# First batch of a threshold attention with a two-layer MLP: the softmax divisors reach x^T through DRAM instead of through TensorE

## The chip, the cores and the metric

The kernel runs on one core of a Trainium2 chip. The metric is the device time of one execution in microseconds (us), as the median of several runs. The core's engines are TensorE (PE; its weight loads are shown apart as PEld), VectorE (DVE), ScalarE (ACT), GpSimd (POOL) and SyncE (SP), which only issues DMA transfers here. ACT and POOL can issue transfers too. Each engine works through its own instructions in order.

## The reference

Attention with 8 batches, 8 heads, 576 positions and 64 channels a head. In each row of scores only those within `tau` of the row's maximum count; the softmax's divisor is the sum over these. The result, with the heads side by side, is the input x (4608 tokens, 512 channels) of an MLP with 2048 hidden channels and an exact GELU.

```python
scores = scale * np.matmul(q, k.transpose(0, 1, 3, 2))
thresh = np.max(scores, axis=-1, keepdims=True) - tau
scores = np.where(scores >= thresh, scores, -1000000000.0)
scores = scores - np.max(scores, axis=-1, keepdims=True)
attn = np.exp(scores)
attn = attn / (np.sum(attn, axis=-1, keepdims=True) + 1e-09)
attn_out = np.matmul(attn, v)
x = attn_out.transpose(0, 2, 1, 3).reshape(B * S, H * D)
h = x @ w_in
out = (0.5 * h * (1.0 + erf(h / sqrt(2)))) @ w_out
```

## The kernel before, in words

Everything is float32. The two heads of a pair stand side by side, so a batch has four pairs and the kernel 32. The 576 query positions of a pair are cut into four chunks of 128 and a tail of 64; the tails of both heads share one chunk, chunk 4.

For each chunk, `scores` (L410) has PE compute scores into PSUM. `softmax_head` takes the negated maximum of each row on DVE (`nmx`, L422), lets POOL work out the threshold (`thr`, L423), and ACT the exponential (`p`, L425). `softmax_tail` has DVE zero what lies below the threshold and sum the rest in the same instruction (L442); the sum goes to `den` in the first batch, and to a column of `sums` later. The exponentials are turned (in the first batch on PE, L356, and copied by ACT, L363; later by DVE and by regrouping transfers on SP, L528 and L524), and `weigh_v` or `weigh_half` multiplies them by v on PE (L545, L569). Its result is x^T: channels on the partitions, tokens along the row. ACT copies it into a block of 256 tokens (`xall`, L555, L571).

So the product with v is taken before the division. The divisors are one per row and lie on the partitions, while x^T has its tokens along the row: they have to be turned, and spread over the 64 channels of a head. The kernel has two ways for that.

In the first batch (`p < EARLY`, pairs 0 to 3) POOL adds 1e-9 to the sums of a chunk (L445), DVE inverts them in the next step (`invert`, L451), and `divide_early` has PE multiply the column, repeated 64 times as the stationary operand, by the identity (L464). ACT copies the outcome from PSUM to `inv` (L466), and POOL multiplies the x^T block by it (L472). `divide_early` runs twice for a pair: for the first 256 tokens (chunks 0 and 1) and for the other 320.

In later batches `divisors` runs once for a pair: DVE adds 1e-9, inverts and turns `sums` (L480, L481, L483), and SP writes the outcome to DRAM (L486) and reads it back, each row repeated on 64 partitions, into `inv` (L492, L494). `divide` multiplies on POOL (L585).

The order of the work is written out by hand in one loop over (pair, chunk) steps. The first batch has 20 steps: first chunks 0 and 1 of pairs 0 to 3, then chunks 2, 3 and 4 of pairs 0 to 3. In each step the scores and the maxima come first, then what is due from earlier steps (weighing and dividing, two steps after the chunk's scores), then matmuls of the MLP as far as `fill` is told to go, then the turns and `softmax_tail`. A division of the first batch therefore stands two steps after the masking that gives its divisors.

Beside this the first batch converts the MLP's weights, which arrive as float64: POOL issues loads of 512 KB pieces (L183), ACT and DVE take the pieces apart (L202, L203, L210, L212), and POOL adds the halves (L226). POOL's queue so holds thresholds, these additions, weight loads and the multiplications by `inv`, in one order. SP's queue holds the loads of q, k and v for the first pairs (L288 to L299), then those of pairs 4 and 5 (`load(HP)` in the last step of pair 1, `load(HP + 1)` three steps ahead of the second batch; L260, L269), and later the regrouping. `load_v_early(p + 2)` stands in the step of chunk 0 of pairs 0 and 1.

`inv` is one buffer (`dg` has one), and so each filling waits until POOL has used the one before.

From about 140 us on there is always an MLP block for PE to fill its gaps with; the last ten blocks are left to the end (L825, `last_blocks`).

Of the kernel before, what the change touches and what calls it, by code (L numbers as in the profile page):

```python
# [8 lines left out]
FP32 = mybir.dt.float32  # L9
# [3 lines left out]
ALU = mybir.AluOpType  # L13
# [5 lines left out]
def kernel(  # L19
# [28 lines left out]
    nc = tc.nc  # L48
    ctx.enter_context(tc.manual_schedule())

    B, H, S, D = q.shape
    d_model, d_ff = moe_w_in.shape
    P = 128
    Q = 32
    HP = H // 2
    NP = B * HP
    EARLY = HP
    NC = S // P
    MAIN = NC * P
    TAIL = S - MAIN  # L60
# [5 lines left out]
    TOK = 256  # L66
# [6 lines left out]
    SLOTS = NC + 1  # L73
# [4 lines left out]
    small = ctx.enter_context(tc.tile_pool(name="small", bufs=4))  # L78
    dram = ctx.enter_context(tc.tile_pool(name="dram", bufs=1, space=bass.MemoryType.DRAM))
    ps = ctx.enter_context(tc.tile_pool(name="ps", bufs=4, space=PSUM))  # L80
# [12 lines left out]
    dg = late_end.enter_context(tc.tile_pool(name="dg", bufs=1))  # L93
# [27 lines left out]
    ident = const.tile([P, P], FP32, name="ident")  # L121
# [122 lines left out]
    st = {}  # L244
# [184 lines left out]
    def softmax_tail(p, i):  # L429

        s = st[p]
        sc, thr, w = s.pop(("sc", i)), s.pop(("thr", i)), s["p", i]
        n = len(sc)
        if p < EARLY:
            pair = small.tile([P, 2], FP32, tag="den", name="den", bufs=2 * SLOTS)
            den = [pair[:, e:e + 1] for e in range(n)]
        else:
            at = [e * NC + i if i < NC else 2 * NC for e in range(n)]
            den = [sums[p % 2][:, x:x + 1] for x in at]
        for e in range(n):  # L440
            row = w[:, e * S:(e + 1) * S].rearrange("p (h s) -> p h s", h=2)
            nc.vector.scalar_tensor_tensor(  # L442
                row, sc[e][:, :, 0:HALF], thr[:, e:e + 1], row, op0=ALU.is_ge, op1=ALU.mult, accum_out=den[e])
        if p < EARLY:
            nc.gpsimd.tensor_scalar(pair[:, 0:n], pair[:, 0:n], 1e-9, None, op0=ALU.add)  # L445
            s["sum", i] = pair[:, 0:n]

    def invert(p, i):

        den = st[p]["sum", i]  # L450
        nc.vector.reciprocal(den, den)  # L451

    def divide_early(p, lo, hi):


        s = st[p]
        b, hp = divmod(p, HP)
        tr = ps.tile([P, 512], FP32, tag="mm", name="tr")
        for i in range(lo // P, -(-hi // P)):
            den = s.pop(("sum", i))  # L460
            to = tr[:, i * P - lo:min((i + 1) * P, hi) - lo]
            for e in range(2):
                one_of, cols = (den[:, e:e + 1], ident) if i < NC else (den, ident[:, e * TAIL:(e + 1) * TAIL])
                nc.tensor.matmul(to[e * D:(e + 1) * D, :], lhsT=one_of.to_broadcast([P, D]), rhs=cols, start=True, stop=True)  # L464
        by = dg.tile([P, S], FP32, tag="inv", name="inv")
        nc.scalar.copy(by[:, 0:hi - lo], tr[:, 0:hi - lo])  # L466
        for n, o, at, size in in_blocks(b, lo, hi):
            x, y = x_blk[n][:, hp, o:o + size], by[:, at - lo:at - lo + size]
            if size == TOK:
                x = x.rearrange("q (p c) -> q c p", c=2)  # L470
                y = y.rearrange("q (c p) -> q c p", c=2)
            nc.gpsimd.tensor_tensor(x, x, y, op=ALU.mult)  # L472

    def divisors(p):

        den = sums[p % 2]
        n = 2 * NC + 1
        nc.vector.tensor_scalar(den[:, 0:n], den[:, 0:n], 1e-9, None, op0=ALU.add)  # L480
        nc.vector.reciprocal(den[:, 0:n], den[:, 0:n])  # L481
        turned = small.tile([P, Q], FP32, tag="turned", name="turned", bufs=2)
        nc.vector.transpose(turned, den)  # L483
        eng = nc.gpsimd if p == NP - 1 else nc.sync
        rows = dram.tile([4, Q, Q], FP32, tag="turned", name="turned", bufs=4)
        eng.dma_start(rows.rearrange("a k i -> (a k) i"), turned)  # L486
        t = st[p]["inv"] = dg.tile([P, S], FP32, tag="inv", name="inv")
        flat = rows.rearrange("a k i -> a (k i)")
        for e in range(2):
            to = t[e * D:(e + 1) * D]  # L490
            src = flat[:, e * P:(e + 1) * P].unsqueeze(0).to_broadcast([D, 4, P])
            eng.dma_start(to[:, 0:MAIN].rearrange("p (a x) -> p a x", x=P), src)  # L492
            src = rows[2 * e:2 * e + 2, 2 * NC, :].unsqueeze(0).to_broadcast([D, 2, Q])
            eng.dma_start(to[:, MAIN:S].rearrange("p (a x) -> p a x", x=Q), src)  # L494
# [596 lines left out]
    for n in range(len(slots) + WEIGH + 1):  # L1091
        p, i = slots[n] if n < len(slots) else divmod(n, SLOTS)
        early = p < EARLY
        last = slots[n - 1] if 0 < n <= len(slots) else None
        if p < NP:
            scores(p, i)
            softmax_head(p, i)
            add_low_bits()
            if last and last[0] < EARLY:
                invert(*last)  # L1100
            if p < HP - 1 and i == 0:
                turn_qk_early(p + 1)
        elif n == len(slots):
            early_end.close()
            weights_first()
        gelus(0)
        if n == BATCH:
            gelus_held()
        table()
        for args in due:  # L1110
            if len(args) == 2:
                weigh_half(*args)
                if args[1]:
                    divide_early(args[0], 0, TOK)
                continue
            weigh_v(*args)
            divide_early(*args)
        due = []
        if p > EARLY and i == WEIGH:
            for lo, hi in (0, WIDE), (WIDE, S):  # L1120
                weigh_v(p - 1, lo, hi)
            if p == NP:
                divide(p - 1)
        owed += (goal(n) - goal(n - 1)) * BLK_NS * (PARTS[i] if not early and p < NP else 1.0)
        if early:
            fill(owed, tokens)
            owed = 0.0
            table()
        if last and last[0] < EARLY and last[1] < NC:
            turn_p_early(*last)  # L1130
        if p < NP:
            softmax_tail(p, i)
        if p < NP and not early:
            turn_p(p, i)
        if p < NP and not early:
            if i == 2:
                regroup(p, 1)
            if i > 2:
                regroup(p, i)
            if i == NC:  # L1140
                divisors(p)
        if last and last[0] < EARLY and last[1] == NC:
            turn_p_early(*last)
        if p < 2 and i == 0:
            for _ in range(2):
                load_piece()
            load_v_early(p + 2)
        if p == 1 and i == NC:
            load(HP)
        if n == BATCH - 3:  # L1150
            load(HP + 1)
        if n == BATCH:
            for t in pd_tail + [turned_p[:, e, h, :, :] for e in range(2) for h in range(2)]:
                nc.gpsimd.memset(t[:, NB:4 * KR, :], 0.0)
        if EARLY < p < NP and i == DIVIDE:
            divide(p - 1)
        if p >= HP and i == 1 and p + 2 < NP:
            loads = load_steps(p + 2)
        if p >= HP:
            next(loads, None)  # L1160
        if p >= HP and i == 1 and p + 1 < NP or p == HP - 1 and i == 2:
            scale_q(p + 1)
        if p >= HP - 1 and i == 2 and p + 1 < NP:
            turn_qk(p + 1)
        convert(0 if n == 0 else 1200 if n < 3 else 1900 if n < BATCH - 1 else 1e9)
        if not early:
            lag[0] = 2 if p < NP else 0
            if n != BATCH:
                share = 0.4 if n == BATCH + 1 else 1.0
                fill(owed * share, tokens)  # L1170
                owed *= 1.0 - share
        if n in BUSY:
            keep_busy(BUSY[n])
        if last and last[0] < EARLY:
            if last[1] < 2 and last[0] in HALVED:
                due.append((last[0], last[1]))
            elif last[1] == 1:
                due.append((last[0], 0, TOK))
            if last[1] == NC:
                due.append((last[0], TOK, S))  # L1180
        if n == START - 1:
            tokens = TOK
        elif n == BATCH + 1:
            tokens = S
        elif p > EARLY and i == DIVIDE and p % HP == 0 or p == NP and i == WEIGH:
            tokens = p // HP * S
            leaving += [n for n in AWAY if n in x_blk and (n + 1) * TOK <= tokens]
        elif leaving and i < 2:
            put_away(leaving.pop(0))
# [35 lines left out]
```

## Time and profile before

| | |
|---|---|
| Time, median of 3 runs | 1340.18 us (1338.49 to 1342.54) |
| The profiled execution | 1340.39 us, span 1338.6 us |
| Busy, share of the span | PE 99%, PEld 67%, DVE 78%, ACT 45%, POOL 49% |
| Chain that ended last | PE 93%, DVE 2%, the rest 1% or less each |
| L464, PE | 80 matmul records of 0.22 to 0.27 us, from 27.0 to 139.0 us |
| L466, ACT | 8 copies, 0.37 to 0.46 us |
| L445, POOL | 20 additions, median 0.30 us |
| L451, DVE | 20 reciprocals, 0.15 us |
| L472, POOL | 12 multiplications, median 0.76 us, from 28.5 to 142.6 us |
| `turned` to DRAM, SP (later batches) | 27 writes, median 1.9 us from issue to landing |
| `inv` from DRAM, SP (later batches) | 108 reads, median 4.0 us from issue to landing |

The span is the profiled execution from its first to its last instruction. A group of the profile names the line, the engine, the operation and the tiles; the chain that ended last follows the work back from the end, at each step to what released it. Times in the trace count from the start of the span.

### The profile page before, as it was taken

The numbers are of one execution on the slowest core, as the hardware profiler recorded it, in microseconds if no ns is written. First come the engines' busy times: TensorE is split into PE (matmuls) and PEld (weight loads), VectorE is DVE, ScalarE is ACT, GpSimd is POOL, SyncE is SP. The second block draws the span as 40 slices with busy tenths as digits, with TensorE's granted clock in tenths as the row PEclk, the third lists the DMA queues.
The fourth block names the chain that finished last, engine by engine and source line by source line (L and its number), as shares of the span: only waits on it lengthen the run. The fifth ranks groups of instructions, "written<-read, shape, count | busy, mean of one in ns | idle before, by whom it ended". The sixth has DMA issues, their size and how long they took to land.

```text
span 1338.6 us, 19954 instructions
## 1 busy us (share of the span) xinstructions
PE 1320.5 (99%) x6354; PEld 893.9 (67%) x6354; DVE 1043.3 (78%) x2005; ACT 604.9 (45%) x1029; POOL 656.0 (49%) x1091
## 2 busy tenths in 40 slices
PE   8899999999999999999999999999999999999998
PEld 6677466466466466457557557568787787877877
DVE  6877778788888888888888888784857698385775
ACT  7877458258357358338438437322211113211120
POOL 5875455555555556545555551245264503635530
PEclk9999999999999999999999999999999999999999
DMA  8652565776786786786787776400000130000003
GB/s 266 190 164 46 121 151 137 166 185 154 173 190 153 176 204 153 176 213 155 164 216 166 162 187 128 108 9 0 1 0 1 38 99 22 1 1 0 1 0 79
DMA packets 209783, 152.41 MB, mean 114 GB/s; under 512 B 113360, under 2 KB 193088, under 8 KB 209680
## 3 DMA queue, kind: packets, MB, share of 16 engines
q1 hardware_dynamic: 187648, 110.43, 36.1%
q0 software_dynamic: 21312, 39.37, 10.7%
q10 hardware_dynamic: 720, 1.34, 0.4%
q8 instruction: 52, 0.85, 0.3%
q14 instruction: 51, 0.42, 0.1%
HBM read 55.97 MB, written 12.52 MB: 51 GB/s over the span
## 4 chain that ended last, share of the span: by engine, by line
PE 93%; DVE 2%; DMA 1%; ACT 1%; POOL 1%; issue 1%; SPq 0%; DVEq 0%; POOLq 0%; ACTq 0%
PE bank L825 34%; PE o_ps L652 17%; PE hT L637 16%; PE sc L410 13%; PE xT L545 12%; DMA q<-in_q_dram 1%; DVE power L212 1%; DMA v<-in_v_dram 1%; POOL w_in L226 1%; DVE nmx L422 0%; PE tr L356 0%; ACT p L425 0%; DVE power L210 0%; ACT pT L363 0%; PE tr L464 0%
## 5 line engine op out<-in xcount | busy, mean ns | idle before, releaser
L425 ACT ACTIVATE p<-sc,nmx 128x576 f32<-128x576 f32 x288 | 201.7, 738 | 275.0 <-DVE nmx L422 274.8
L442 DVE SCALAR_TENSOR_TENSOR p<-sc,thr,p 128x576 f32<-128x576 f32 x288 | 226.4, 816 | 78.1 <-ACT p L425 68.2
L423 POOL TENSOR_SCALAR thr<-nmx,tau_eff 128x1 f32<-128x1 f32 x288 | 84.5, 293 | 359.8 <-DVE nmx L422 350.3
L637 PE MATMUL hT<-xall,w_in 128*128 128x256 f32 x1024 | 242.0, 386 | 0.2 <-POOL xall L472 0.2
L422 DVE TENSOR_REDUCE nmx<-sc 128x1 f32<-128x576 f32 x288 | 205.4, 750 | 43.7 <-PE sc L410 42.4
L652 PE MATMUL o_ps<-w_out,g 128*128 128x512 f32 x512 | 236.8, 603 | 0.0
L637 PEld LDWEIGHTS hT<-xall,w_in 128*128 128x128 f32 x1024 | 189.3, 190 | 50.5 <-issue 23.0
L707 DVE TENSOR_TENSOR c<-c,bank 128x320 f32<-128x320 f32 x304 | 147.0, 487 | 33.8 <-PE bank L825 20.5
L707 DVE TENSOR_TENSOR o<-o,bank 128x256 f32<-128x256 f32 x240 | 99.8, 419 | 93.7 <-PE bank L825 88.7
L652 PEld LDWEIGHTS o_ps<-w_out,g 128*128 128x128 f32 x512 | 93.1, 190 | 109.1 <-issue 106.3
L410 PE MATMUL sc<-kT,qT 64*128 64x288 f32 x960 | 161.3, 429 | 2.6 <-DVE p L442 2.6
L545 PE MATMUL xT<-pT,v 128*64 128x320 f32 (+1 forms) x1240 | 159.6, 409 | 0.7 <-DVE pT L367 0.5
L506 DVE STREAM_TRANSPOSE turned_p<-p 128x1152 f32<-128x1152 f32 x112 | 154.4, 1378 | 3.9
L410 PEld LDWEIGHTS sc<-kT,qT 64*128 64x128 f32 x960 | 91.8, 186 | 77.2 <-issue 62.5
L545 PEld LDWEIGHTS xT<-pT,v 128*64 128x64 f32 x1240 | 86.5, 137 | 71.5 <-issue 10.8
L825 PE MATMUL bank<-w_out,c 128*128 128x256 f32 x480 | 120.2, 381 | 0.5 <-DVE o L707 0.5
L269 POOL DMA_DIRECT2D v<-in_v_dram x208 | 110.9, 536 | 4.1 <-issue 2.2
L825 PEld LDWEIGHTS bank<-w_out,c 128*128 128x128 f32 x480 | 89.9, 190 | 18.8 <-DVE o L707 3.0
L878 ACT ACTIVATE c<-c 128x320 f32<-128x320 f32 (+1 forms) x80 | 46.9, 624 | 114.6 <-DVE c L707 114.5
L707 POOL TENSOR_TENSOR c<-c,g 128x320 f32<-128x320 f32 (+1 forms) x40 | 50.5, 1271 | 67.5 <-DVE c L707 67.5
L825 PE MATMUL bank<-t_out,c 128*128 128x256 f32 x320 | 82.8, 381 | 0.0
L825 PE MATMUL bank<-t_out,g 128*128 128x256 f32 x320 | 82.1, 379 | 0.0
(184 smaller groups left out, 1785.5 us busy)
## 6 DMA issues: line engine op xcount, KB each, us to landing
pT<-turned_p SPq DMA_DIRECT2D x448, 160.0 KB, 3.6
pT<-pd_tail SPq DMA_DIRECT2D x112, 80.0 KB, 2.9
q<-in_q_dram POOLq DMA_DIRECT2D x104, 72.0 KB, 3.6
k<-in_k_dram POOLq DMA_DIRECT2D x104, 72.0 KB, 3.1
inv<-turned SPq DMA_DIRECT2D x54, 128.0 KB, 4.0
v<-in_v_dram POOLq DMA_DIRECT2D x156, 40.0 KB, 3.0
out_dram<-o SPq DMA_DIRECT2D x40, 128.0 KB, 2.3
xall<-in_moe_w_out_dram POOLq DMA_DIRECT2D x9, 512.0 KB, 4.2
```

The source lines that it names most:

```text
L269: eng.dma_start(t[r:P:4, e, 0:n, :], rows[:, r * KR:r * KR + n, :])
L410: nc.tensor.matmul(sc[e][:, h, 0:HALF], lhsT=lhsT, rhs=s["kT"][rows, at:at + HALF], start=True, stop=True)
L422: nc.vector.tensor_reduce(nmx[:, e:e + 1], sc, axis=AXIS.XY, op=ALU.max, negate=True)
L423: nc.gpsimd.tensor_scalar(thr[:, e:e + 1], nmx[:, e:e + 1], -1.0, tau_eff, op0=ALU.mult, op1=ALU.subtract)
L425: nc.scalar.activation(w[:, e * S:(e + 1) * S].rearrange("p (h s) -> p h s", h=2), sc, AF.Exp, bias=nmx[:, e:e + 1], scale=1.0)
L442: nc.vector.scalar_tensor_tensor(row, sc[e][:, :, 0:HALF], thr[:, e:e + 1], row, op0=ALU.is_ge, op1=ALU.mult, accum_out=den[e])
L506: nc.vector.transpose(turned_p[:, :, i // 2, 0:NB, i % 2 * Q:(i % 2 + 1) * Q], w.rearrange("p (e b i) -> p e b i", e=2, i=Q))
L545: nc.tensor.matmul(to, lhsT=s["v"][:, e, c, :], rhs=rhs, start=(c == 0), stop=(c == KR - 1))
L637: nc.tensor.matmul(hT[:, j % 2, :], lhsT=w_in_sb[c][:, j * P:(j + 1) * P], rhs=x_blk[n][:, c, :], start=(c == 0), stop=(c == N_DM - 1))
L652: nc.tensor.matmul(o[:, 0:d_model], lhsT=g[j][:, m * P:(m + 1) * P], rhs=w_out_sb[j], start=(j == 0), stop=(j == N_DF - 1))
L707: eng.tensor_tensor(out, a, b, op=ALU.add)
L825: nc.tensor.matmul(to, lhsT=l, rhs=r, start=start and k == 0, stop=k == len(pairs) - 1, skip_group_check=not start)
```

## The change

In the first batch the sums go to `sums`, as in later batches. `invert` and its call are gone, as are POOL's addition and, in `divide_early`, the matmuls and the copy. After `softmax_tail` of chunks 1 and 4 of a pair, `divisors` is called with a chunk number: DVE adds, inverts and turns the nine columns, SP writes them to DRAM and reads back those of chunks 0 and 1 (two reads), or of chunks 2, 3 and 4 (four reads). `divide_early` finds `inv` filled and multiplies; the view of x^T in that multiplication follows the other order in which the divisors arrive. The steps in which the divisions stand are the same.

```diff
     def softmax_tail(p, i):
...
-        if p < EARLY:
-            pair = small.tile([P, 2], FP32, tag="den", name="den", bufs=2 * SLOTS)
-            den = [pair[:, e:e + 1] for e in range(n)]
-        else:
-            at = [e * NC + i if i < NC else 2 * NC for e in range(n)]
-            den = [sums[p % 2][:, x:x + 1] for x in at]
+        at = [e * NC + i if i < NC else 2 * NC for e in range(n)]
+        den = [sums[p % 2][:, x:x + 1] for x in at]
...
-        if p < EARLY:
-            nc.gpsimd.tensor_scalar(pair[:, 0:n], pair[:, 0:n], 1e-9, None, op0=ALU.add)
-            s["sum", i] = pair[:, 0:n]
-
-    def invert(p, i):
-        den = st[p]["sum", i]
-        nc.vector.reciprocal(den, den)
-
     def divide_early(p, lo, hi):
-        s = st[p]
         b, hp = divmod(p, HP)
-        tr = ps.tile([P, 512], FP32, tag="mm", name="tr")
-        for i in range(lo // P, -(-hi // P)):
-            den = s.pop(("sum", i))
-            to = tr[:, i * P - lo:min((i + 1) * P, hi) - lo]
-            for e in range(2):
-                one_of, cols = (den[:, e:e + 1], ident) if i < NC else (den, ident[:, e * TAIL:(e + 1) * TAIL])
-                nc.tensor.matmul(to[e * D:(e + 1) * D, :], lhsT=one_of.to_broadcast([P, D]), rhs=cols, start=True, stop=True)
-        by = dg.tile([P, S], FP32, tag="inv", name="inv")
-        nc.scalar.copy(by[:, 0:hi - lo], tr[:, 0:hi - lo])
+        by = st[p].pop("inv")
         for n, o, at, size in in_blocks(b, lo, hi):
...
             if size == TOK:
-                x = x.rearrange("q (p c) -> q c p", c=2)
-                y = y.rearrange("q (c p) -> q c p", c=2)
+                x = x.rearrange("q (a i c) -> q a c i", i=Q, c=2)
+                y = y.rearrange("q (a c i) -> q a c i", i=Q, c=2)
             nc.gpsimd.tensor_tensor(x, x, y, op=ALU.mult)
 
-    def divisors(p):
+    def divisors(p, chunk=None):
...
         for e in range(2):
             to = t[e * D:(e + 1) * D]
+            if chunk is not None:
+                src = flat[:, (e * NC + chunk) * Q:(e * NC + chunk + 2) * Q]
+                eng.dma_start(to[:, 0:TOK].rearrange("p (a x) -> p a x", x=2 * Q),
+                              src.unsqueeze(0).to_broadcast([D, 4, 2 * Q]))
+                if chunk:
+                    src = rows[2 * e:2 * e + 2, 2 * NC, :].unsqueeze(0).to_broadcast([D, 2, Q])
+                    eng.dma_start(to[:, TOK:TOK + TAIL].rearrange("p (a x) -> p a x", x=Q), src)
+                continue
...
-            if last and last[0] < EARLY:
-                invert(*last)
...
         if p < NP:
             softmax_tail(p, i)
+        if early and i in (1, NC):
+            divisors(p, 0 if i == 1 else 2)
```

## The prediction

> **What bounds the kernel now.** I read first the page's busy shares and its chain that ended last: TensorE (PE) is 99% busy and 93% of the chain. So everywhere but in the first batch a microsecond counts only on PE, and the change touches the first batch alone, some 140 us. There I read the chain in order of time. I number its 20 steps 0 to 19: steps 0 to 7 are chunks 0 and 1 of pairs 0 to 3, steps 8 to 19 chunks 2 to 4. From about 76 us the chain is PE with short stretches of VectorE (DVE) and ScalarE (ACT); the divisor matmuls L464 are on it. Ahead of that it changes between PE, ACT, DVE and GpSimd (POOL), and each hands on to the next with little slack. In these lines (start, length, engine) see the four late L464 groups, and a POOL stretch that holds `den` L445:
>
> ```profile
> 53.07 0.92 POOL xall L472
> ...
> 54.08 0.83 POOL den L445
> ...
> 56.19 0.33 POOL thr L423
> ...
> 79.54 0.55 PE tr L464 x12
> ...
> 99.08 0.55 PE tr L464 x12
> ...
> 119.53 0.55 PE tr L464 x12
> ...
> 138.56 0.71 PE tr L464 x10
> ```
>
> PE fills its gaps with work in an order fixed by the program, so time lost early is not made up later: after 150 us PE has no gap to take it up. A delay in the first batch goes to the end nearly whole.
>
> **What decides, I think, is the first division.** It is the POOL multiply L472 at 28.55 us in step 3. The timeline of POOL shows what stands behind it: two weight loads L183, then the thresholds L423 of step 4, for which DVE's masking L442 waits. In the second fence DVE starts its two maskings at 33.01 and 33.95.
>
> ```profile
> 28.55 0.74 POOL L472 TENSOR_TENSOR xall<-xall,inv 128x256 f32<-128x256 f32 x1 [0.64 <-ACT inv L466]
> 29.37 0.84 POOL L445 TENSOR_SCALAR den<-den 128x2 f32<-128x2 f32 x1
> 30.27 0.65 POOL L183 DMA_DIRECT2D xall<-in_moe_w_in_dram  x1
> 31.20 0.53 POOL L183 DMA_DIRECT2D turned_p<-in_moe_w_in_dram  x1 [0.28 <-DVE power L212]
> 32.09 0.31 POOL L423 TENSOR_SCALAR thr<-nmx,tau_eff 128x1 f32<-128x1 f32 x1 [0.36 <-DVE nmx L422]
> ```
>
> ```profile
> 33.01 0.82 DVE L442 SCALAR_TENSOR_TENSOR p<-sc,thr,p 128x576 f32<-128x576 f32 x1 [0.37 <-ACT p L425]
> ...
> 33.95 0.82 DVE L442 SCALAR_TENSOR_TENSOR p<-sc,thr,p 128x576 f32<-128x576 f32 x1
> ```
>
> SyncE's queue (SP) is not free then. The new transfers stand behind the load of pair 2's v, whose last two issues are the first two lines here; the third is pair 3's v, which they displace:
>
> ```profile
> 25.21 0.51 SPq L298 DMA_DIRECT2D v<-in_v_dram  x1
> 25.76 0.47 SPq L299 DMA_DIRECT2D v<-in_v_dram  x1
> 26.27 0.78 SPq L298 DMA_DIRECT2D v<-in_v_dram  x1
> ```
>
> The answer for tile v, cut to the first two of these, gives their time to landing:
>
> ```profile
> DMA to landing us min/median/max: 7.5/7.6/7.8
> ```
>
> So they land at 32.7 and 33.6. The table by stretches has the DMA engines 0.94 busy from 25 to 30 us.
>
> **What the skill says.** The Trainium skill, "DMA: Bandwidth & Descriptors", section "Queues, rings and completion order": each DMA engine takes turns between queues packet by packet, a ring is drained in order, and the completion write lands only after that engine's earlier writes. The trace agrees: v of 16 KB takes 7.8 us here, behind 512 KB weight pieces that POOL issued at 24.4, 25.0 and 25.5, and v of 24 KB 2.5 us between 90 and 130. Its section "Two DMAs through the same engine are not ordered" has the issuing engine wait for the first of two dependent transfers; in the second batch SP waits 1.3 us (L492 for `turned`). "TensorE: Matmul & The Clock Gate", Part 1, lets the clock halve after an idle window of about 3.4 us; at the start of this trace the 128-column matmuls take 0.42 us, later 0.27.
>
> **The change part by part.**
>
> *PE loses L464* (80 records of 0.27, overlapped). On the chain the four late groups are 3 x 0.55 + 0.71 = 2.4 us; taken whole: **-2.4**. The groups at 27.3 and 38.8 are 0.64 each on the chain; the first is covered by the wait below, the second by ACT's work, so 0; bare, they would give another 1.3.
>
> *ACT loses 8 copies L466* (0.37 to 0.46). Not on the chain, though ACT is busy 28.1 of 30 us from 30 to 60. I take **-0.5**, since ACT gets ahead and the waits of L442 for ACT (0.37, 0.67) go; at most 4 x 0.4 = 1.6.
>
> *POOL loses 20 additions L445* (0.23 to 0.89). Most end before the next maximum is there. In step 8 the threshold starts at 56.19, though its maximum was there at 55.55: **-0.6**. The multiply keeps its size with another view; same duration taken, +-0.2 each.
>
> *DVE loses 20 reciprocals L451* (0.15), and gains 8 times addition, reciprocal and turn of 128x9 and 128x32. In the second batch these run from 160.14 to 160.69: 0.55 each, 4.4 in all. The reciprocals mostly stood before a masking that waited for ACT or POOL, so I credit only 0.3. Four of the additions (steps 10, 13, 16, 19) follow maskings where DVE is on the chain or within 0.1 us: 4 x 0.45 - 0.3 = **+1.5** (0 to 3).
>
> *SP gains 8 writes and 24 reads* (two reads for a first half, four for a second). For step 1: DVE's turn is done by 19, but SP gets there at 26.27. The write lands behind v: 33.6 + 0.4 = 34.0. SP waits for it, then issues two reads, 0.6 each, the second at 34.7. Landing 4.0, the page's median for `inv`: 38.7. POOL multiplies until 39.5, issues two loads (1.2) and starts the threshold at 40.7 where it was 32.09. The second threshold ends 1.85 later, at 42.6 (1.85: threshold, addition L226, threshold), and the second L442 follows at 42.6 where it was 33.95: +8.7. Since POOL's next two loads are held back, the queue empties somewhat sooner: **+8.0**. Bounds: if the write overtakes (1.9, the page's median) and the reads take 3.1, they are in at 32.0, the second L442 at 35.8: +1.9. If the write lands like the v at 26.27 (9.4) and the reads take 5.8: 42.2, or +12.2. PE stands idle some 6 us then; should its clock halve, 0 to +1.5, taken as 0.
>
> *The other seven divisions.* In step 3 the write now stands behind pair 3's v; it and its reads are in at about 45, with POOL there at 48 (40.07 + 8). For steps 5 and 7 the way is write 0.6, landing about 2.5, reads 1.3, landing 4: 8.4 us from DVE's end at 40.4 and 52.7, against multiplies at 53.07 and 65.09; 4 us to spare. For the second halves, with four reads, 9.5 us from 70.2, 89.0, 108.8 and 128, against 81.7, 101.1, 122.7 and 141.9: 2 to 4 to spare. They cost 0, covered by the two steps between masking and multiply; uncovered, a few us each.
>
> *Moved on SP:* q and k of pair 4 (L260, issued from 29 to 42 before) now stand behind step 13's divisors, at about 95 to 101 plus the shift. ACT scales that q at 115.44; about 10 us to spare. Pair 5's q, k and v end near 125, the first regrouping L528 is at 143.78. Both 0.
>
> Sum: +8.0 - 2.4 - 0.5 - 0.6 + 1.5 = **+6.0**. The profiled execution took 1340.39 (span 1338.6), as good as the median of the runs, 1340.18; from that, **1346.2 us**.
>
> **The rivals.** *The first wait is short, and all but cancels* (chance 0.22): the write gets through among the weights' packets, as with +1.9 to +6: the sum is -0.1 to +4.0, 1340 to 1344. For it: 16 KB are little, and `turned` lands in 1.9 later. Against: the 16 KB v took 7.8. *Faster* (0.10): PE is what bounds, and the transfer is hidden. That needs both reads landed by about 30 us, 1.5 us after POOL gets there, for POOL has that much slack with L445 gone. Then 0 instead of +8, and the early L464 may count: -2.0 to -4.8, 1335.4 to 1338. Against it is SP's place at 26.27: even the quickest landings give 32.0. *Every division waits* (0.08): if landings stay at 7 us under weight loads (7.6 for one at 36.2), the spare 4 us are gone in steps 5 and 7, with 2 to 3 us each: 1351 to 1354. That the change doesn't do what it says is no rival: the order of instructions shows L464, L445, L451 and L466 gone.
>
> **How the numbers follow.** The main case (first wait +6 to +12; chance 0.60) spans 1344 to 1352, of which 0.02 falls under 1344.2. About 0.3%, 4 us, is what a measurement can tell from no change. Slower: 0.58 + 0.08 = 0.66; same 0.24; faster 0.10. The range 1338 to 1353 takes in the main case, the short wait and the edge of the others.
>
> **What would show it.** In the profile after: POOL idle some 10 us before its first multiply by `inv`, released by SP's read; the first SP write near 26.3, landing past 32; DVE idle about as long in step 4; PE's hT start near 64.7 shifted by 6 to 9 us; later multiplies with no wait; the shift at 145 us some 2 us less. The prediction is wrong if POOL's first wait is under 4 us, or if the multiplies in steps 5 to 21 wait too.

## The result, and the profile after

The changed kernel is slower: 1353.36 us, the median of 6 runs (1352.83 to 1354.63), against 1339.24 us before (6 runs, 1337.23 to 1342.54) on the same chip. The ratio is 1.0104, with a 95% interval of 1.0092 to 1.0116. That is 14.1 us, where +6.0 was forecast; the time lies 0.4 us above the range. The profiled execution took 1354.63 us, with a span of 1352.9.

Where the 14 us arise is read by laying the start of the same matmuls in both traces side by side. Up to 64 us the changed kernel falls back by 9.1 us; from there to 156 us by 2.0 more; between 680 and 720 us by some 3. Everything else is level.

**The first 45 us.** POOL's timeline has the first multiply, the second threshold of step 3 ahead of it, and behind it what it held back. In brackets stand the idle time before an instruction and what the profile takes for its releaser:

```profile
26.80 0.28 POOL L423 TENSOR_SCALAR thr<-nmx,tau_eff 128x1 f32<-128x1 f32 x1
38.78 0.74 POOL L450 TENSOR_TENSOR xall<-xall,inv 128x256 f32<-128x256 f32 x1 [11.69 <-DMA v<-in_v_dram]
39.46 0.62 POOL L183 DMA_DIRECT2D xall<-in_moe_w_in_dram  x1
40.08 0.53 POOL L183 DMA_DIRECT2D turned_p<-in_moe_w_in_dram  x1
40.65 0.31 POOL L423 TENSOR_SCALAR thr<-nmx,tau_eff 128x1 f32<-128x1 f32 x1
```

The multiply starts at 38.78 instead of 28.55, after 11.69 us idle. The releaser is inferred and names v. But the multiply's own operand, `inv`, is in by 38.6, just before it starts. SP's queue:

```profile
24.73 1.38 SPq L298 DMA_DIRECT2D v<-in_v_dram  x1
...
27.51 0.59 SPq L299 DMA_DIRECT2D v<-in_v_dram  x1
29.34 0.33 SPq L466 DMA_DIRECT2D turned<-turned  x1
34.29 1.27 SPq L473 DMA_DIRECT2D inv<-turned  x2
```

The first write issues at 29.34, 3.1 us later than I had it: SP reaches the four v issues ahead of it 0.9 us later than before, they take 1.0 us more, and then SP stands for 1.2 us, which the profile puts down to v's transfer. SP waits until the write has landed (4.9 us by the trace's answer for the tile) and issues the reads from 34.29 on; they land within 3.6 us. The two loads and the threshold of step 4 come after the multiply, so DVE's maskings of step 4 stand where the threshold lets them, at 40.99 and 42.48:

```profile
40.99 0.82 DVE L438 SCALAR_TENSOR_TENSOR p<-sc,thr,p 128x576 f32<-128x576 f32 x1 [8.34 <-POOL thr L423]
...
42.48 0.82 DVE L438 SCALAR_TENSOR_TENSOR p<-sc,thr,p 128x576 f32<-128x576 f32 x1 [0.66 <-POOL thr L423]
```

TensorE waits for these maskings, and what it does next runs slowly:

```profile
41.87 1.32 PE L410 MATMUL sc<-pd_tail,qT 64*128 64x288 f32 x2 [7.02 <-DVE p L438]
43.36 2.28 PE L410 MATMUL sc<-pd_tail,qT 64*128 64x288 f32 x6 [0.16 <-DVE p L438]
45.57 3.34 PE L533 MATMUL xT<-pT,v 128*64 128x256 f32 x20
...
49.98 1.24 PE L410 MATMUL sc<-pd_tail,qT 64*128 64x288 f32 x8
```

Before, the same x^T and what follows it up to the scores of step 6:

```profile
36.23 2.64 PE L545 MATMUL xT<-pT,v 128*64 128x256 f32 x19
...
38.72 0.81 PE L464 MATMUL tr<-ident,den 128*64 128x128 f32 x6
...
40.58 1.24 PE L410 MATMUL sc<-pd_tail,qT 64*128 64x288 f32 x8
```

The table by stretches gives the clock; its columns are the length, the busy time of PE, PEld, DVE, ACT and POOL with their counts, then the granted clock, the DMA share and GB/s:

```profile
39.00:42.00 3.00, 0.13 (x1) 0.13 (x1) 0.82 (x2) 0.00 (x0) 2.96 (x5) 0.50 0.44 94
42.00:45.00 3.00, 2.84 (x8) 1.54 (x8) 2.48 (x5) 0.00 (x0) 1.90 (x4) 0.50 0.89 305
45.00:48.00 3.00, 3.00 (x16) 1.50 (x16) 2.46 (x6) 1.41 (x2) 2.18 (x4) 0.57 0.51 164
```

From the second masking to the scores of step 6 it is 7.50 us after and 6.63 before. So the halved clock costs 0.9 us net, on top of the wait; before, a group of L464, 0.64 us on the chain, stood in the same stretch.

**Around step 18.** The chain, in order of time, goes through DVE's addition of the new divisors, an instruction that the first batch did not have before:

```profile
117.29 0.84 DVE p L438 x2
118.12 0.02 issue
118.15 1.26 DVE sums L460
119.41 0.02 issue
119.43 0.23 DVE sums L461
```

L460 takes 1.25 us here; in five of its eight places in the first batch it takes 0.17. The maximum L422 follows late, then ACT's exponential and its copy of g (a part of an MLP block, ahead of the GELU). PE waits 1.57 us for that, and the scores take 2.58 us; the granted clock is 0.50 to 0.53 from 126 to 129 us:

```profile
124.63 0.33 PE L356 MATMUL tr<-ident,p 128*128 128x128 f32 x1 [1.57 <-ACT g L592]
124.88 2.58 PE L410 MATMUL sc<-pd_tail,qT 64*128 64x288 f32 x8
```

Before, PE waits 0.78 us there, the scores take 1.97, and the clock is 1.00 from 112 to 122 us:

```profile
114.47 0.33 PE L356 MATMUL tr<-ident,p 128*128 128x128 f32 x1 [0.78 <-ACT g L604]
114.73 1.97 PE L410 MATMUL sc<-pd_tail,qT 64*128 64x288 f32 x8
```

**At 703 us** ScalarE's copy into a slot of x waits 6.94 us for the transfer by which `put_away` moves a finished block of x^T from that slot to DRAM (before, 4.96 in the same place, which was covered). PE then waits 2.02 us, and its clock falls to 0.56 to 0.58 from 706 to 710 us.

The sum by traces: 9.1 + 2.0 + 3.0 = 14.1, against spans that differ by 14.3.

### The profile page after: what moved, and what is told of

The parts are those of the page before. It is cut to its first block, busy times and chain, and to the rows that moved or that the text cites. A ratio compares the mean times of both kernels' runs of the same rounds, so it can differ in the third digit from the quotient of the medians.

```text
span 1352.9 us, 19831 instructions
## 1 busy us (share of the span) xinstructions
PE 1320.4 (98%) x6274; PEld 891.0 (66%) x6274; DVE 1045.8 (77%) x2009; ACT 602.6 (45%) x1021; POOL 645.3 (48%) x1071
## 3 DMA queue, kind: packets, MB, share of 16 engines
q1 hardware_dynamic: 194304, 111.75, 36.8%
q0 software_dynamic: 21312, 39.37, 10.4%
## 4 chain that ended last, share of the span: by engine, by line
PE 88%; DVE 1%; DMA 1%; ACT 1%; issue 0%; SPq 0%; POOL 0%; DVEq 0%; ACTq 0%; POOLq 0%
PE bank L813 34%; PE o_ps L640 16%; PE hT L625 15%; PE sc L410 12%; PE xT L533 10%; DMA x<-xall 1%; ACT p L425 1%; DVE p L438 0%; DVE nmx L422 0%; DMA turned<-turned 0%; DVE power L212 0%; DVE power L210 0%; PE tr L356 0%; DVE sums L460 0%; DVE turned_p L494 0%
## 5 line engine op out<-in xcount | busy, mean ns | idle before, releaser
L422 DVE TENSOR_REDUCE nmx<-sc 128x1 f32<-128x576 f32 x288 | 205.3, 750 | 45.0 <-PE sc L410 43.8
L533 PEld LDWEIGHTS xT<-pT,v 128*64 128x64 f32 x1240 | 87.1, 138 | 72.9 <-issue 13.8
```

The costliest lines, as they stand in the source:

```text
L422: nc.vector.tensor_reduce(nmx[:, e:e + 1], sc, axis=AXIS.XY, op=ALU.max, negate=True)
L533: nc.tensor.matmul(to, lhsT=s["v"][:, e, c, :], rhs=rhs, start=(c == 0), stop=(c == KR - 1))
```

## The experiments

I reckoned that the first wait and what follows from it is most of the loss. The rival was that DVE's and SP's added work, spread over all eight divisions, costs it. Every kernel is timed against the kernel before on the same chip. The table holds how far each profiled execution is behind the profiled execution of before at the same matmul: the scores of step 2 (17.8 us before), of step 10 (63.7), of step 19 (124.2), of step 24 (155.8), and two later scores. One trace each, so these are worth about as much as two executions of one kernel differ: the second trace of before starts 2.5 us later and keeps that to its end.

| kernel | 17.8 | 63.7 | 124.2 | 155.8 | 565.9 | 845.6 | ratio (interval) |
|---|---|---|---|---|---|---|---|
| changed | -0.8 | 9.1 | 11.2 | 11.1 | 11.4 | 14.2 | 1.0104 (1.0092, 1.0116) |
| only the first moved | 3.1 | 9.3 | 9.3 | 9.3 | 10.4 | 9.6 | 1.0081 (1.0066, 1.0096) |
| all but the first | -1.0 | -0.3 | 3.5 | 3.4 | 3.7 | 5.7 | 1.0042 (1.0027, 1.0057) |
| v behind the divisors | -0.5 | 8.8 | 11.0 | 12.5 | 12.9 | 13.8 | 1.0089 (1.0072, 1.0107) |
| first multiply late | 1.3 | 6.5 | 8.6 | 9.9 | 10.3 | 11.0 | 1.0068 (1.0054, 1.0083) |
| all but the first, DVE relieved | -0.1 | 1.0 | 0.3 | 1.3 | 1.6 | 1.0 | 1.0024 (1.0017, 1.0030) |
| queue cleared | -0.3 | 6.3 | 6.7 | 6.6 | 6.9 | 8.3 | 1.0073 (1.0060, 1.0086) |
| kept busy | 0.1 | 8.6 | 12.2 | 12.1 | 12.4 | 11.9 | 1.0094 (1.0078, 1.0111) |
| two multiplies late, DVE relieved | -1.4 | 0.0 | -0.6 | 1.4 | 1.8 | 3.7 | 1.0036 (1.0026, 1.0046) |
| second halves only, DVE relieved | -1.0 | -0.1 | -0.7 | 2.4 | 2.5 | 1.5 | 1.0020 (1.0012, 1.0027) |
| changed, once more | -0.4 | 9.5 | 11.6 | 12.8 | 13.2 | 15.8 | one run |
| before, once more | 2.5 | 2.6 | 2.6 | 2.6 | 2.6 | 2.5 | one run |

### Only the first division through DRAM

The kernel before, in which both ways exist side by side and this decides:

```diff
+    def through_dram(p, i):
+        return p < EARLY and p == 0 and i < 2
```

> The kernel before, with one pair's divisors (pair 0, first half: the first division of all) taken through DRAM, and the other seven divisions left on TensorE. Theory 1 (the first wait and what comes of it is most of the loss): GpSimd idles about 10 us before its first multiply, TensorE about 7 us before the scores of step 5 and then runs some steps at a halved clock; about +9 to +10 us over the kernel before, near 1349. If the later shift of some 3 us at 700 us of the changed kernel is a consequence of where everything then lies, +12 to +13. Rival (the loss is VectorE's added instructions and SyncE's added issues, spread over all eight divisions): an eighth of it, +1 to +2 us, near 1341.

1350.86 us (before 1339.46), ratio 1.0081: one division of eight, alone, costs about four fifths of the loss (11.4 of 14.1 us by the medians). That is theory 1; a spread loss would have given +1 to +2. The traced execution began 3.1 us later than that of before, and still POOL's multiply started at 37.58, not later than in the changed kernel; so POOL stood idle for 5.85 us here, not for 10. From 64 us on it loses only some tenths: no drop at step 18.

### All but the first

```diff
+        return p < EARLY and (p > 0 or i >= 2)
```

> The change with one part undone: pair 0's first division keeps its way through TensorE, the other seven go through DRAM. Theory 1: no long wait of GpSimd or TensorE in the first 60 us; what is left is VectorE's added work against TensorE's 16 x 8 fewer small matmuls, and the drop of the clock near 124 us; +1 to +3 us over the kernel before, 1340 to 1343. Rival (spread over all eight): seven eighths of the loss, about +12 us, near 1351.

1346.22 us, ratio 1.0042: +6.8 us by the medians, +5.6 by the ratio, more than the 1 to 3 of theory 1 and about half of the rival's 12. With the kernel above that makes 18.2 us by the medians, more than the 14.1 of both together: the parts don't add up. The long wait is gone (-0.3 at 64 us), as expected, though pair 1's multiply, now the first through DRAM, waits 2.5 us for its reads. But 3.5 us come between 104 and 124 us, and 2 more at put_away. The first of these is plain in the trace. In DVE's timeline of step 16, the addition L492 is held for 1.1 us while POOL runs its two additions of the weights' low bits; POOL's line comes second:

```profile
108.77 1.25 DVE L492 TENSOR_SCALAR sums<-sums 128x9 f32<-128x9 f32 x1
110.06 0.21 DVE L493 RECIPROCAL sums<-sums 128x9 f32<-128x9 f32 x1
110.30 0.21 DVE L495 STREAM_TRANSPOSE turned<-sums 128x32 f32<-128x32 f32 x1
```

```profile
107.49 2.49 POOL L226 TENSOR_TENSOR w_out<-power,w_out 128x512 uint32<-128x512 uint32 x2
```

The addition ends when POOL's do, at 110.0. Before, a DVE instruction of the weights' conversion stood in that place and paid it (0.69 us elsewhere):

```profile
109.12 1.65 DVE L212 SCALAR_TENSOR_TENSOR power<-xall,power 128x512 uint32<-128x512 uint32 x1
```

So the stall is not new, but with three instructions more on DVE the maximum of step 17 starts at 112.53 instead of 111.75. PE's wait for g then grows from 0.78 to 1.57 us, and the clock falls to 0.50 to 0.52 from 116 to 122 us; the same scores take 3.00 us:

```profile
115.25 0.33 PE L356 MATMUL tr<-ident,p 128*128 128x128 f32 x1 [1.57 <-ACT g L624]
115.51 3.00 PE L410 MATMUL sc<-pd_tail,qT 64*128 64x288 f32 x8
```

The Trainium skill ("SBUF — State Buffer", "Who interferes with whom") has DVE and GpSimd share one pair of ports as an exclusive lock, which a DVE `tensor_scalar` in its two-port form takes; the loser waits for the whole instruction. The 1.25 against 0.17 us, and the common end, agree with that.

### DVE relieved in those steps

The kernel above, and in three of the four steps that make a second half's divisors (10, 13 and 16; step 19 converts whatever is left) 700 ns less of the weights' conversion, given back two steps later:

```diff
+        shift = {10: -700, 12: 700, 13: -700, 15: 700, 16: -700, 18: 700}.get(n, 0)
-        convert(0 if n == 0 else 1200 if n < 3 else 1900 if n < BATCH - 1 else 1e9)
+        convert(0 if n == 0 else 1200 if n < 3 else 1900 + shift if n < BATCH - 1 else 1e9)
```

> The kernel with seven divisions through DRAM (pair 0's first on TensorE), with one more edit: in each step that makes the divisors of a second half, VectorE gets 700 ns less of the weights' conversion, and as much more two steps later, so that its three added instructions displace conversions and not the maximum of the next step. Theory (VectorE's 0.6 us put the scores' maximum of step 17 0.78 us later, TensorE's wait for g grows from 0.78 to 1.57 us, and the clock falls to 0.51): step 17 as in the kernel before, no drop of the clock, 3 to 3.5 us less than without the edit, so 1341 to 1343. Rival (the clock falls because the small matmuls for the divisors are gone, not because VectorE is late): the clock drops as before, within 1 us of 1346.

1343.05 us (20 runs; before 1339.83), ratio 1.0024: 3.5 us less than without the edit by the medians, 2.4 by the ratios. The wait is 0.52 us, the scores are quick again and the clock holds, though the small matmuls are gone all the same:

```profile
115.27 0.33 PE L356 MATMUL tr<-ident,p 128*128 128x128 f32 x1 [0.52 <-ACT g L624]
115.53 1.95 PE L410 MATMUL sc<-pd_tail,qT 64*128 64x288 f32 x8
```

So it was DVE's lateness that let the clock fall, and not the want of those matmuls. But the longer wait only makes the fall likely. Eight of the fourteen traces taken have 1.57 or 1.58 us of wait at step 18; the clock falls in six of them and holds in two, one of which is "queue cleared":

```profile
121.76 0.33 PE L356 MATMUL tr<-ident,p 128*128 128x128 f32 x1 [1.57 <-ACT g L592]
122.02 1.95 PE L410 MATMUL sc<-pd_tail,qT 64*128 64x288 f32 x8
```

In the six traces with 0.51 to 0.78 us it holds. What decides between the eight was not tried.

### What the landing depends on

First v behind the divisors:

```diff
         if p < 2 and i == 0:
             for _ in range(2):
                 load_piece()
-            load_v_early(p + 2)
+        if p < 2 and i == 1:
+            load_v_early(p + 2)
```

> The changed kernel, with the v loads of pairs 2 and 3 issued on SyncE behind the first divisors' transfers and not ahead of them. Theory 1, with the queue ahead as the reason for the late landing: the first write issues some 3 us earlier and lands in about 2 us and not 4.9, so GpSimd's first multiply starts some 5 us earlier than 38.8 us; about 5 us less than the changed kernel, near 1348. Rival (the three transfers in a row cost their 3 to 5 us each whatever lies ahead of them in the queue): at most 2 us less, near 1352.

1352.53 us, ratio 1.0089: 1 us less than the changed kernel by the medians, each against its own before, and 2 by the ratios, so the rival's number. (Its six runs lie from 1349.02 to 1354.98, and the trace is of one at 1354.29.) But its reason isn't right either. The write issued 4.9 us earlier than in the changed kernel and landed 1.3 us earlier, as SP's read at 32.99 shows; it took 8.5 us where 4.9 were enough there:

```profile
24.42 1.35 SPq L466 DMA_DIRECT2D turned<-turned  x1
32.99 1.27 SPq L473 DMA_DIRECT2D inv<-turned  x2
```

In three kernels the write issued at 24.42, 26.93 (only the first moved) and 29.34, and the multiply started at 37.32, 37.58 and 38.78. The second of them, the one that began late, shows best what holds the transfers up: its write issued ahead of three weight pieces (28.16 to 29.31) and had landed after 2.4 us, and its reads behind them took 7.4 to 7.8 us, where the changed kernel's took 3.4 to 3.6. Then also two of the four 512 KB pieces of weights that POOL issues from 20 to 25 us, held back behind that multiply:

```diff
-        if p < 2 and i == 0:
+        if n == 0 or n == 3:
             for _ in range(2):
                 load_piece()
```

> The changed kernel with v of pairs 2 and 3 behind the first divisors on SyncE (as above, where that alone left the write landing at 33 us) and with the two 512 KB pieces of weights that GpSimd issues in step 2 held back to step 3, behind the first multiply. Theory (the first write lands when the transfers issued ahead of it, weights above all, have drained): issued near 24.4 us, it lands by 30 and not at 33, and GpSimd's first multiply starts by 34 to 35 and not at 37.3 to 38.8; 3 to 4 us less at the 64 us mark, if the later pieces aren't missed. Rival (a write, its completion and two reads cost this long by themselves): landing as before, no gain.

```profile
24.55 0.53 SPq L466 DMA_DIRECT2D turned<-turned  x1
28.53 1.27 SPq L473 DMA_DIRECT2D inv<-turned  x2
```

With 1 MB less ahead, the same write landed in 4.0 us, and POOL's multiply started at 33.72, as expected. 1350.51 us, ratio 1.0073, some 3 to 4 us less than the changed kernel. Of the 5.1 us by which the multiply came earlier, 2.8 are left at 64 us. So the landing depends above all on the weights that another queue has outstanding, as the theory has it; SP's own order changed it by 1.3 us.

### The multiply late, the transfers as they are

> The changed kernel with only the first multiply moved: pair 0's first half is divided by GpSimd two steps later, at the start of step 5, out of a buffer of its own, so that nothing on GpSimd waits for the first transfers; every transfer, every VectorE instruction and every missing TensorE matmul stays as in the changed kernel. Theory 1 (what the wait held back behind it on GpSimd, the thresholds of step 4, is the loss): no wait, 9 to 10 us less than the changed kernel, near 1343. Rival (the transfers themselves, or VectorE's added work, cost the time): no more than 2 us less, near 1352.

In this first try pair 0's reads landed in `pd_tail[1]`, to which pair 3's k is turned before the multiply uses them, so its x^T of that half is multiplied by k and not by the inverse. It takes 1349.78 us, but PE waits 3.8 us for ACT's turn of that k, so it says nothing on the theory.

The second, with the reads in an unused part of `turned_p`:

```diff
+            t = st[p]["inv0"] = pd[1][:, 4 * PIECE:5 * PIECE]
...
             weigh_v(*args)
-            divide_early(*args)
+            if args[:2] != (0, 0):
+                divide_early(*args)
+        if n == 5:
+            divide_early(0, 0, TOK)
```

> The changed kernel with only the first multiply moved two steps later, to the start of step 5, this time with the reads landing in a part of turned_p that nothing uses before step 20 (in the kernel above they landed in the buffer that pair 3's k is turned into, and that turn waited 3.8 us for them). Transfers, VectorE's work and the missing TensorE matmuls stay as in the changed kernel. Theory (what the wait holds back on GpSimd is 9 us of the loss; a further 3 to 4 us come at step 18, where VectorE is late and the clock drops; about 1 to 3 at the end of put_away): the first mark at 64 us no more than 1 us behind the kernel before, the whole 9 to 10 us less than the changed kernel, 1342 to 1345. Rival (the transfers or VectorE's work cost it whatever waits for them): no more than 3 us less, near 1351.

1349.26 us, ratio 1.0068: 4.7 us less than the changed kernel by the medians, not the 9 to 10 that I expected, and more than the rival's 3. Pair 0's multiply waits for nothing of its own. But pair 1's, which now stands just ahead of it in POOL's order, does:

```profile
48.21 0.74 POOL L450 TENSOR_TENSOR xall<-xall,inv 128x256 f32<-128x256 f32 x1 [6.65 <-ACT pT L363]
48.92 0.73 POOL L450 TENSOR_TENSOR xall<-xall,turned_p 128x256 f32<-128x256 f32 x1
```

```profile
38.48 0.53 SPq L466 DMA_DIRECT2D turned<-turned  x1
43.63 1.27 SPq L476 DMA_DIRECT2D inv<-turned  x2
```

The releaser named, ACT, had long been done: the reads issue from 43.63 on and are in by 48.0. The write takes 5.2 us with the weights moving on, where it takes 2.0 in the changed kernel, whose POOL holds back the next weights meanwhile. But there too the reads are not in before 46.2, and POOL, 9.4 us late by then, reaches this multiply only at 49.46. Here it would have been there at 41.6. The first wait had covered the second, mostly by making POOL late.

So both multiplies late (steps 5 and 7), each from a buffer of its own, with DVE relieved as above. All eight divisions go through DRAM:

```diff
-            if args[:2] != (0, 0):
+            if args[0] > 1 or args[1] > 0:
                 divide_early(*args)
-        if n == 5:
-            divide_early(0, 0, TOK)
+        if n in (5, 7):
+            divide_early((n - 5) // 2, 0, TOK)
```

> The changed kernel (all eight divisions through DRAM) with the first halves of pairs 0 and 1 both multiplied two steps later, at steps 5 and 7, out of parts of turned_p that are unused so early, and with VectorE's conversions shifted by 700 ns away from the four steps that make second halves' divisors. With the first multiply alone moved, the wait was found again at the second (6.65 us at 41 to 48 us). Theory (GpSimd's in-order wait for transfers that take 8 to 10 us in the first 50 us, and step 18's clock, are the whole loss): no multiply waits over 1 us, the 64 us mark within 1.5 us of the kernel before, total 1339 to 1343. Rival (the wait moves on again, to the third division, or transfers slow the loads): 1345 or more.

1345.19 us, ratio 1.0036; at 64 us level with the kernel before (it had begun 1.4 us earlier), and no multiply waits over 0.2 us for its reads:

```profile
38.85 0.73 POOL L450 TENSOR_TENSOR xall<-xall,turned_p 128x256 f32<-128x256 f32 x1
52.79 0.74 POOL L450 TENSOR_TENSOR xall<-xall,inv 128x256 f32<-128x256 f32 x1 [0.19 <-DMA inv<-turned]
53.50 0.93 POOL L450 TENSOR_TENSOR xall<-xall,turned_p 128x256 f32<-128x256 f32 x1
```

This shows it for the first 64 us: the transfers cost nothing there once nothing on POOL stands behind them. The total is the rival's number, 2 us over mine, but not by the rival's third wait: 2.0 us come between 124 and 156 us, where PE waits 1.64 us for DVE at step 21 and the clock falls, and 1.9 at put_away.

### Second halves only

```diff
+        return p < EARLY and (i >= 2)
```

with the shift of the conversions.

> Only the four second halves through DRAM (the four first halves' divisors stay on TensorE), with the same shift of VectorE's conversions. Theory (second halves have ample time, TensorE saves 12 small matmuls each, 4 x 0.55 us where it waits for nothing): no wait of a multiply, the 130 us mark 0 to 2 us ahead of the kernel before, total 1337.5 to 1340. Rival (VectorE's three added instructions cost TensorE what it saves, wherever they stand): 1340 to 1343, as with seven divisions moved.

1343.38 us (22 runs; before 1340.22), ratio 1.0020: just above the rival's range. It is level with the kernel before at 104 us, although two groups of L464 are gone by then, and 0.7 us ahead at 124. At step 21 PE waits 1.65 us for DVE, 0.15 before, and the clock halves again:

```profile
133.48 0.72 PE L410 MATMUL sc<-kT,qT 64*128 64x288 f32 x2 [1.65 <-DVE p L445]
134.60 2.26 PE L410 MATMUL sc<-kT,qT 64*128 64x288 f32 x6 [0.40 <-DVE p L445]
```

Without the shift this wait is 0.59. By step 19 all conversions have to be done, so what DVE puts off comes back there. Here too the wait alone does not decide: with seven divisions moved and DVE relieved, PE waits 1.63 us in this place and the clock stays at 1.00. No version that I tried beats the kernel before.

### Idle matmuls

```diff
-    BUSY = {6: 2, 8: 2, BATCH: 4}
+    BUSY = {4: 14, 6: 2, 8: 2, 17: 4, BATCH: 4}
```

> The changed kernel with idle matmuls of 128 columns on TensorE: 28 at the end of step 4, where it waits 7 us, and 8 at the end of step 17. Nothing else is changed. Theory (of the loss of the first 50 us about 1 us is TensorE at half clock after its wait, and near 124 us some 1.7 more): the clock stays at 1.0 in 42 to 48 us, 1 us less at the 64 us mark, up to 2.6 us less at the end, 1351 to 1353. Rival (the idle matmuls take as much time as they save, or the clock falls all the same): within 0.5 us of the changed kernel.

1352.87 us, ratio 1.0094: the same as the changed kernel within the intervals. Part of it worked: the clock is 1.0 from 42 us, x^T takes 2.38 us instead of 3.34, and step 6 comes 1.0 us earlier, although the idle matmuls ran on to 44.4 us and held up the scores of step 5. But those of step 17 stand behind PE's wait for g and run at the low clock; the scores of step 18 come 3.2 us later than in the changed kernel, and step 19 1.0 us later. The gain is given back.

### Both kernels once more

> The changed kernel once more, for a second trace. If the 3 us that it lost between 680 and 720 us (ScalarE's copy waiting 6.9 us for put_away's read of x) belong to it, they are there again at the same place; if they are how transfers happened to land in that execution, they are elsewhere or smaller, as in the six variants of it (-0.1 to +2.3 us).

> The kernel before once more, for a second trace: how far the marks of one and the same kernel lie apart between two executions (1 us or so expected from the start), and whether put_away costs it anything when it falls otherwise.

1356.29 and 1342.91 us. The changed kernel loses 1.5 us near 590 and 1.4 near 690 at put_away, so 3 us again, but in two places. Its score matmuls, from 565 to 725 us, wait 3.0 and 3.8 us for DVE in its two traces; the kernel before 0.9 and 1.2 in its two. The ten variants gain or lose anything from -1.0 to +2.0 between 566 and 846 us. So it comes with the change more often than not, but what decides it I can't say: after 160 us both kernels do the same work.

## Why the prediction was wrong

**The direction and the main mechanism were right, the size wasn't.** Slower by the first wait, up to the end, with the places that I named: POOL idle before its first multiply (11.7 us for "some 10"), DVE idle in step 4 (8.3), and the other multiplies without a wait for transfers in the changed kernel. The kernels with the first undone and with both multiplies late show that this wait is the largest cause: at 64 us they are level with the kernel before, where the changed kernel is 9.1 behind. In whole times undoing the first is worth some 7 us by the medians (14.1 - 6.8) and 8 by the ratios. By the traces, 8.1 us more were lost than forecast: 2.2 up to 64 us, 2.9 from there to 156, and 3.0 at put_away.

**SP's first write and reads, +8.0.** The raw sum was +8.7; the second masking came 8.5 later by the clock and 9.3 measured from step 2, which began 0.8 earlier. Two errors in it cancelled: the write issued at 29.3 and not at 26.3, and landed in 4.9 us, not in 7.7. What failed is the discount of 0.7 for a queue that empties sooner. Nothing of it is seen in the first transfers: the multiply started at 38.78, and the raw sum had 38.7. With POOL's -0.6 and ACT's -0.5, of which nothing is seen at 64 us, 6.9 was forecast there and 9.1 measured.

**"Should its clock halve, 0 to +1.5, taken as 0."** It halved, for 0.9 us net. The price was in the text and the lower end chosen. The Trainium skill ("TensorE: Matmul & The Clock Gate", Part 1) has the clock halve after an idle window of about 3.4 us; PE's 7.02 idle microseconds hold one. At step 18, though, no idle stretch is that long: the clock fell after a wait of 1.57 us (in the kernel with seven moved, PE was busy 2.43 us of the 4 from 112 to 116), and it held after the same wait with the queue cleared (2.43 us of the 4 from 120 to 124). The idle window as stated does not cover that.

**DVE, +1.5, and PE's -2.4.** PE did lose L464 (12 matmuls gone in each of the late four), but from 64 to 156 us the kernel lost 2.0 instead of gaining 0.9. The sign of a shift 2 us smaller at 145 us did not come: it was 11.1 there. DVE's three instructions cost more than my 0.45 where POOL's addition holds theirs (1.25 us for the one), and their lateness stretches a wait after which the clock can fall: 3.5 us in the kernel with seven moved, of which 0.8 is the wait. I had summed the edit by durations, and did not ask what the longer wait would do to PE.

**"The other seven divisions cost 0."** True in the changed kernel. For pair 1's the prediction had counted on the first wait: reads in at 45, POOL there at 48, which was 8 us late; they were in at 46.2, and POOL was there at 49.46. What it did not draw from this is that without the first wait the second one comes: with the first multiply late, pair 1's waits 6.65 us. The rival had the first halves of pairs 2 and 3 wait too; with both multiplies late, neither of them waits over 0.2 us.

**Put_away** is in no step of the prediction: "time lost early is not made up later" was right, but that nothing is added later, which the sum took for granted, was not. Those 3 us stay open.

## What to carry to other kernels

An in-order engine's wait for a transfer costs what stands behind it. Place the use where the whole round trip has been measured under the load of that moment, and ask what the wait itself had been holding back, since curing one wait can lay bare the next. Taking small work off the bounding engine brings nothing when its neighbour with little slack takes it over: here 0.8 us of VectorE's lateness became 1.8 us in the changed kernel and 3.5 with seven divisions moved, where TensorE's clock fell after the longer wait.

## What the runs showed of the hardware

- Small dependent transfers behind 512 KB weight pieces of another queue came in late almost whenever they were issued: with the write at 24.4, 26.9 or 29.3 us, the divisors were used at 37.3, 37.6 and 38.8; with 1 MB of weights held back and the write at 24.6, at 33.7.
- A DVE addition on nine columns took 0.17 us in the five of eight places where no GpSimd instruction but DMA issues ran beside it (changed kernel). In the other three it took 0.37, 1.08 and 1.25 us and ended within 0.04 us after GpSimd's.
- After a wait of 1.57 us at step 18 TensorE's granted clock fell to some 0.5 in six of eight traces; after 0.51 to 0.78 us it held in six of six. At step 21 it fell after 1.65 us in one kernel and held after 1.63 in another.
